# The first batch's value loads put behind the fourth unit's queries and keys

## The chip, the core and the metric

The kernel runs on one core of a Trainium2 chip. The metric is device time in microseconds (us) of one launch; lower is better. The core's engines are TensorE (PE; its weight loads are shown as PEld), VectorE (DVE), ScalarE (ACT), GpSimd (POOL) and SyncE (SP). SP issues all the transfers between the device memory and the core here, in the order of its queue, and sixteen DMA engines carry them.

## The reference

Windowed attention, and then a feed-forward layer with a maximum over three products:

```python
scores = q @ k.T / 8                       # 8 batches, 8 heads, 576 positions, 64 wide
# heads 0-3 see the last 32 positions; heads 4-7 every fourth of the last 128
attn = exp(masked - max) / (sum + 1e-9)
x = (attn @ v) as 4608 tokens x 512
h = max(x @ w1, x @ w2, x @ w3)            # 512 -> 768
out = h @ w_out                            # 768 -> 512
```

All is float32 with tight accuracy, so each product of the feed-forward layer is made of three: a high part and a low part of each operand are used (high times high, low times high, high times low).

## The kernel before, in words

**Units.** Attention is done in units of two heads: 8 batches of 4 units, `p` 0 to 3; `p` 0 and 1 are plain windows, 2 and 3 dilated. The first batch takes them in the order `PORDER = (2, 0, 3, 1)`, so the fourth unit is `p` 1. The first six units go through `full(b, p)`, the later ones through `attention` and `behind`. In names, `02` is batch 0, unit `p` 2, and `10` is batch 1, unit 0.

A unit of `full` loads its queries and keys (`fk`; the unit 03 has them in two, `fk` and `fq`) and its values (`fv`, two loads). On PE come the scores (`fs`, lines 576 and 582), transposes of the weights of attention (`ft`, 666 and 690) and the product with the values (`fpv`, 712). Between them ACT and DVE do the softmax, POOL multiplies by the reciprocal of the sum, and ACT copies the transposed tiles. At the end ACT and DVE write the unit's part of `x` as a high part `xH` and a low part `xL`.

**Weights.** The up weights are 18 pieces `st0` to `st17` of 512 KB, the down weights `st18` to `st24`. Each is loaded (line 473) and then split into high and low parts: ACT makes `cp` from `st` (446), POOL makes `c` from `st` (453), DVE joins them (459, 467), ACT writes `wupH` and POOL or DVE writes `wupL`. Piece `j` serves the group `u0_f_g` with `j = 3f + g`.

**Feed-forward.** Nine tiles of 512 tokens. A tile has 18 groups of 12 matmuls `u` (line 1021), which go in turn to two PSUM banks. The first of three groups is copied to `tmp` by ACT (`copy`, line 361), the next two are taken into the maximum by DVE (line 387); each of these frees the group's bank. ACT and POOL split the maximum into `h`. Then come 72 matmuls `d` (1092), and the output goes out (1121). In the first tile two groups, `u0_0_0` and `u0_0_1`, are done on three quarters of `x` before the fourth unit is ready, and then finished.

**What sets the order.** All steps are given to a `Plan`. `Plan.order` is a list scheduler: it has a cost for each step, a rate for the wire and due times, picks the next step of each engine, and so fixes the order of every engine's instructions and of SP's loads. A step becomes ready when the steps that it depends on have ended in the plan (`left` counts them, `next` lists who is waiting). `fill` steps are matmuls on zeros (line 1200, `idle`), put where the plan sees PE with nothing to do; the plan reckons with a slower PE after a stretch of little work (`TICK`, line 30, and lines 229 to 236). The instructions are then issued in that order, and each engine's queue is in that order. The waits on the chip come from data and buffers: a DMA that writes a buffer waits for the last reader, and an instruction waits for the landing of what it reads.

Queries and keys have two buffers (`k`) and the ones of unit 03 stand in two of six `h` buffers; the first batch's values take `h` buffers too. The pieces `st0` to `st22` use six `wd` buffers in turn.

Of the kernel before, what the change touches and what calls it, by code (L numbers as in the profile page):

```python
# [36 lines left out]
PORDER = (2, 0, 3, 1)  # L37
# [256 lines left out]
def tile_dilated_window_attention__then__maxout_ffn(  # L294
# [205 lines left out]
        return s, l, first  # L500


    first_of = [None] * (FULL + 1)

    def full(b, p):
# [18 lines left out]
        def load(dst, src, rows, n):  # L524
            return {"sp": 0.5}, lambda _: nc.sync.dma_start(out=dst.t[:rows, :n], in_=src), (), [dst], rows * n * 4 * PART[rows]

        if at_h:
            ks = plan.add(*load(kb, qk[b, p % 2, :, 576:], 128, nkc))
            heads = []
            qs = plan.add(*load(qb, qk[b, p % 2, :, :576], 128, 576))  # L530
        else:
            ks = qs = None
            heads = []
            heads.append(plan.add(*load(kb, qk[b, p % 2], 128, 576 + nkc)))
        if b:
            vs = []
            for i in range(2):
                n = at[i + 1] - at[i]

                def values_in(_, i=i, n=n):  # L540
                    dst = vb[i].t[:wk, : 2 * n * D].rearrange("p (j c) -> p j c", j=2)
                    nc.sync.dma_start(out=dst, in_=fv[b, p % 2, :, :, at[i] * D : at[i + 1] * D].rearrange("j p c -> p j c"))

                vs.append(plan.add({"sp": 0.5}, values_in, (), [vb[i]], wk * 2 * n * D * 4 * PART[wk]))
        else:
            vs = [plan.add(*load(vb[j], fv[b, p % 2, j], wk, 64 * nblk)) for j in range(2)]

        def value(n, j):

            if not b:  # L550
                return vb[j].t[:wk, D * n : D * n + D]
            i = n // 6
            c = D * (j * (at[i + 1] - at[i]) + n - at[i])
            return vb[i].t[:wk, c : c + D]
# [625 lines left out]
    for n in TILES:  # L1180
        plan.kind = "a"
        while HALF * 2 * (u // NPAIR) < t0 + n:
            for p in range(NPAIR):
                if u < FULL_UNITS:
                    plan.lead = UNIT_LEAD * (NPAIR - 1 - p)
                    x_of.extend(full(u // NPAIR, p if u >= NPAIR else PORDER[p]))
                else:
                    n_u = 1 if u < ALONE else 2
                    if u < ALONE or u % 2 == 0:
                        units(range(u, u + n_u))  # L1190
                u += 1
        plan.kind = "ffn"
        prev, last_up = ffn(t0, n, x_of, w_of, prev)
        readers.append((t0, t0 + n, last_up))
        t0 += n
# [72 lines left out]
```

## Time and profile before

| | |
|---|---|
| median of 3 runs | 687.71 us (687.3 to 687.76) |
| the profiled execution | 688.23 us, of which the span of instructions is 686.4 us |
| PE busy | 678.7 us, 99% of the span (the matmuls on zeros count as busy) |
| DVE, ACT, POOL busy | 335.3, 251.7, 179.5 us |
| moved by DMA | 55.43 MB; q1, SP's queue, 54.53 MB |

The profile's second part cuts the span in 40 slices of about 17 us and gives the busy share of each in tenths. Its timeline lists instructions with start, duration, engine, line, operation, output and inputs, and in brackets the idle time ahead of it and what ended it. A group of equal instructions on one engine is one row with a count.

### The profile page before, as it was taken

The page shows a single profiled execution, that of the slowest core. Times are in us where ns is not written, and L with a number is a line of the kernel's source. Part 1 is how long each engine was busy: PE and PEld are TensorE (multiplying, and loading weights), DVE is VectorE, ACT ScalarE, POOL GpSimd, SP SyncE. Part 2 cuts the span into 40 slices and gives each one's busy share as a digit, 9 for nine tenths or more (in the row PEclk, how much of TensorE's full clock was granted, in tenths as well). Part 3 has the DMA queues.
Part 4 walks back from the last instruction along what each step waited for, and adds up shares of the span by engine and source line. Part 5 has one row for each costly group of instructions (what it writes and reads, how often), then busy time and mean ns, then how long its engine had stood idle before and what let it go on. Part 6 is the DMA issues. An engine that isn't in the chain of part 4 may idle for free.

```text
span 686.4 us, 13901 instructions
## 1 busy us (share of the span) xinstructions
PE 678.7 (99%) x5458; PEld 552.1 (80%) x5458; DVE 335.3 (49%) x1194; ACT 251.7 (37%) x867; POOL 179.5 (26%) x228
## 2 busy tenths in 40 slices
PE   8999999999999999999999999999999999999997
PEld 5678778888888888888888888888888888888886
DVE  6879867786787675112765257614611211101110
ACT  5857665526534534112641254314311211111111
POOL 2657852323223412111232111311211001100110
PEclk9999999999999999999999999999999999999999
DMA  9997343141433123001610051101000000010001
GB/s 289 310 344 245 103 138 114 48 121 44 139 115 115 44 67 116 1 0 40 214 37 8 1 186 68 44 0 56 32 1 1 34 28 0 1 47 15 1 0 62
DMA packets 20690, 55.43 MB, mean 81 GB/s; under 512 B 2128, under 2 KB 6224, under 8 KB 20624
## 3 DMA queue, kind: packets, MB, share of 16 engines
q1 hardware_dynamic: 20624, 54.53, 24.0%
q8 instruction: 43, 0.70, 0.4%
q14 instruction: 23, 0.19, 0.1%
HBM read 45.09 MB, written 9.44 MB: 79 GB/s over the span
## 4 chain that ended last, share of the span: by engine, by line
PE 91%; DMA 4%; DVE 1%; POOL 1%; ACT 1%; issue 1%; SPq 0%; DVEq 0%; ACTq 0%; POOLq 0%
PE u L1021 60%; PE d L1092 22%; DMA st<-in_w_up_dram 4%; PE s L826 3%; PE pv L986 3%; PE idle L1200 1%; POOL W L387 1%; PE fpv L712 1%; PE ft L666 1%; ACT wupH L361 0%; DVE cp L459 0%; ACT cp L446 0%; DVE tmp L387 0%; DVE cp L467 0%; POOL h L387 0%
## 5 line engine op out<-in xcount | busy, mean ns | idle before, releaser
L387 DVE TENSOR_TENSOR tmp<-u,tmp 128x512 f32<-128x512 f32 x108 | 74.6, 691 | 251.8 <-PE u L1021 242.1
L1021 PE MATMUL u<-xH,wupH 128*128 128x512 f32 x648 | 175.3, 392 | 0.7 <-ACT tmp L361 0.5
L1021 PE MATMUL u<-xL,wupH 128*128 128x512 f32 x648 | 174.4, 391 | 0.0
L1021 PE MATMUL u<-xH,wupL 128*128 128x512 f32 x648 | 174.3, 390 | 0.0
L387 POOL TENSOR_TENSOR h<-tmp,h 128x512 fp32r<-128x512 f32 x54 | 69.9, 1295 | 322.9 <-ACT h L361 322.8
L1092 PE MATMUL d<-wdn,h 128*128 128x512 f32 x648 | 152.9, 393 | 0.0
L1021 PEld LDWEIGHTS u<-xH,wupH 128*128 128x128 f32 x648 | 120.7, 188 | 26.8 <-ACT tmp L361 1.4
L1021 PEld LDWEIGHTS u<-xL,wupH 128*128 128x128 f32 x648 | 121.2, 188 | 25.5
L1021 PEld LDWEIGHTS u<-xH,wupL 128*128 128x128 f32 x648 | 121.3, 188 | 25.3
L1092 PEld LDWEIGHTS d<-wdn,h 128*128 128x128 f32 x648 | 120.5, 188 | 26.0
L930 DVE STREAM_TRANSPOSE PT<-W 32x256 f32<-32x256 f32 (+2 forms) x320 | 120.2, 376 | 25.0 <-PE pv L986 9.7
L361 ACT CAST h<-tmp 128x512 fp32r<-128x512 f32 x54 | 33.5, 621 | 211.2 <-DVE tmp L387 211.2
L876 ACT ACTIVATE W<-W,mx 128x96 f32<-128x96 f32 x260 | 93.6, 364 | 22.2 <-DVE mx L864 19.5
L387 POOL TENSOR_TENSOR W<-W,sm 128x768 f32<-128x768 f32 (+2 forms) x52 | 49.6, 959 | 28.3 <-DVE sm L905 27.3
L361 ACT COPY tmp<-u 128x512 f32<-128x512 f32 x54 | 31.7, 586 | 67.0 <-POOL h L387 37.7
L864 DVE CUSTOM_DVE_ANT_0 W<-s,steps 128x96 f32<-128x96 f32 (+1 forms) x232 | 44.1, 252 | 12.0 <-PE s L826 11.6
L876 ACT ACTIVATION_READ_ACCUMULATOR W<-W,mx 128x1 f32 x260 | 49.5, 190 | 0.0
L361 ACT COPY o<-d 128x512 f32<-128x512 f32 (+1 forms) x36 | 21.0, 582 | 75.4 <-PE d L1092 64.2
L900 POOL TENSOR_TENSOR sm<-sm,small_c 128x8 f32<-128x8 f32 (+2 forms) x52 | 10.0, 196 | 108.6 <-ACT W L876 108.5
L361 ACT CAST xH<-pv 128x288 fp32r<-128x288 f32 (+8 forms) x70 | 20.2, 346 | 29.0 <-PE u L1021 20.8
L387 DVE TENSOR_TENSOR xL<-pv,xH 128x288 fp32r<-128x288 f32 (+8 forms) x70 | 23.0, 374 | 10.0 <-ACT xH L361 9.5
L986 PEld LDWEIGHTS pv<-PT,v 64*64 64x64 f32 x1152 | 22.1, 134 | 4.9 <-issue 4.6
(69 smaller groups left out, 350.6 us busy)
## 6 DMA issues: line engine op xcount, KB each, us to landing
st<-in_w_up_dram SPq DMA_DIRECT2D x18, 512.0 KB, 9.7
k<-in_qk_d_dram SPq DMA_DIRECT2D x14, 648.0 KB, 4.4
out_dram<-o SPq DMA_DIRECT2D x35, 256.0 KB, 2.0
k<-in_qk_p_dram SPq DMA_DIRECT2D x12, 592.0 KB, 4.3
v<-in_vw_d_dram SPq DMA_DIRECT2D x14, 384.0 KB, 3.3
v<-in_vw_p_dram SPq DMA_DIRECT2D x12, 320.0 KB, 3.7
st<-in_w_dn_dram SPq DMA_DIRECT2D x5, 512.0 KB, 4.5
fk<-in_qk_p_dram SPq DMA_DIRECT2D x4, 592.0 KB, 8.2
```

The source lines that it names most:

```text
L361: nc.scalar.copy(dst, src)
L387: (nc.vector if eng == "dve" else nc.gpsimd).tensor_tensor(dst, a, b, op=op)
L666: nc.tensor.transpose(flips[j].t[:wk, gw * g : gw * g + gw], W3(j)[:gw, g], ident[:gw, :gw])
L712: nc.tensor.matmul(pv[z].t[64 * j : 64 * j + 64, c : c + nq], value(n, j), turned(j, x, x + nq), start=True, stop=True,)
L826: nc.tensor.matmul(banks[j].t[o : o + nq, 96 * m : 96 * m + nk], kb.t[d, q0 : q0 + nq], kb.t[d, k0 : k0 + nk], start=True, stop=True,)
L864: nc.vector.tensor_tensor_reduce(W.t[rows, a], banks[j].t[rows, 96 * m : 96 * m + nk], mask_of(m)[rows], -0.125, 3e38, ALU.add, ALU.min, m ...
L876: nc.scalar.activation(W.t[rows, a], W.t[rows, a], AF.Exp, bias=mx.t[rows, n : n + 1], scale=-1.0, accum_out=sm.t[rows, n : n + 1],)
L900: nc.gpsimd.tensor_tensor(d, d, eps_c[rows].broadcast_to([d.shape[0], n]), op=ALU.add)
L930: plan.add({"dve": dve(32 * n) + 0.02}, lambda _: nc.vector.transpose(dst(), src()), [*deps, blank], [W, PT])
L986: nc.tensor.matmul(pv[z].t[64 * j : 64 * j + 64, q : q + c1 - c0], v.t[d, j, y], PT.t[d, 576 * j + 96 * x + c0 : 576 * j + 96 * x + c1], s ...
L1021: nc.tensor.matmul(sums(bank), wt[:, j, c, :], moving(xL if xz else xH, c), start=(m == 0 and c == EARLY[0]), stop=(m == 2 and c == EARLY[3]),
L1092: nc.tensor.matmul(bank.t, hs[f].t[:, hz, s0 : s0 + 128], wdn[f].t[:, wz], start=(f == 0 and m == 0), stop=(f == NF - 1 and m == 2),)
```

## The change

`full` collects the value loads of the first batch's four units. When the fourth unit (`p == PORDER[3]`) is added, each of these eight loads is made to depend, in the plan, on the load of that unit's queries and keys (`heads[0]`). The dependence is the plan's; no wait is written for the chip, beyond those of data and buffers.

```diff
+    first_vs = []
     first_of = [None] * (FULL + 1)
 
     def full(b, p):
...
         else:
             vs = [plan.add(*load(vb[j], fv[b, p % 2, j], wk, 64 * nblk)) for j in range(2)]
+            first_vs.extend(vs)
+            if p == PORDER[3]:
+                for st in first_vs:
+                    heads[0].next.append(st)
+                    st.left += 1
```

In rows of the changed kernel, lines 504 to 546 have become one higher, and those behind the change six higher.

The start of SP's queue, before (names end in a running number; `fk02` is 648 KB, an `fv0` load 240 or 216 KB, an `st` 512 KB):

```order
L525 DMA fk02_111<-in_qk_d_dram 128x1296
L525 DMA fk00_113<-in_qk_p_dram 128x1184
L525 DMA fv02_0_115<-in_fv_d_dram 80x768
L525 DMA fv02_1_121<-in_fv_d_dram 80x768
L525 DMA fk03_123<-in_qk_d_dram 128x720
L525 DMA fq03_165<-in_qk_d_dram 128x576
L525 DMA fv00_0_167<-in_fv_p_dram 96x576
L525 DMA fv00_1_195<-in_fv_p_dram 96x576
L525 DMA fk01_198<-in_qk_p_dram 128x1184
L473 DMA st0_207<-in_w_up_dram 128x512
L473 DMA st1_255<-in_w_up_dram 128x512
L525 DMA fv03_0_267<-in_fv_d_dram 80x768
```

And now:

```order
L526 DMA fk02_111<-in_qk_d_dram 128x1296
L526 DMA fk00_113<-in_qk_p_dram 128x1184
L526 DMA fk03_115<-in_qk_d_dram 128x720
L526 DMA fq03_121<-in_qk_d_dram 128x576
L473 DMA st0_123<-in_w_up_dram 128x512
L473 DMA st1_165<-in_w_up_dram 128x512
L526 DMA fk01_193<-in_qk_p_dram 128x1184
L473 DMA st2_229<-in_w_up_dram 128x512
L473 DMA st3_240<-in_w_up_dram 128x512
L473 DMA st4_247<-in_w_up_dram 128x512
L526 DMA fv02_0_294<-in_fv_d_dram 80x768
L526 DMA fv02_1_302<-in_fv_d_dram 80x768
```

Five pieces of the up weights and the fourth unit's queries and keys now stand ahead of the first values. The loads of `fv00`, `fv03`, `st5`, `fk10`, `fv01` and `fk11` follow, up to the 21st load, and behind them SP's queue differs a second time. Before, from the 22nd load on:

```order
L473 DMA st6_484<-in_w_up_dram 128x512
L542 DMA fv10_0_492<-in_fv_p_dram 96x2x384
L473 DMA st7_533<-in_w_up_dram 128x512
L473 DMA st8_552<-in_w_up_dram 128x512
L542 DMA fv10_1_569<-in_fv_p_dram 96x2x192
L473 DMA st23_573<-in_w_dn_dram 128x256
L473 DMA st24_581<-in_w_dn_dram 128x256
L473 DMA st9_606<-in_w_up_dram 128x512
```

Now, from the 22nd on:

```order
L473 DMA st6_474<-in_w_up_dram 128x512
L543 DMA fv10_0_518<-in_fv_p_dram 96x2x384
L473 DMA st7_526<-in_w_up_dram 128x512
L543 DMA fv10_1_545<-in_fv_p_dram 96x2x192
L473 DMA st23_550<-in_w_dn_dram 128x256
L473 DMA st24_565<-in_w_dn_dram 128x256
L543 DMA fv11_0_575<-in_fv_p_dram 96x2x384
L473 DMA st8_604<-in_w_up_dram 128x512
L473 DMA st9_614<-in_w_up_dram 128x512
```

`st8` moved from the 25th place to the 29th: `fv10_1`, `st23`, `st24` and `fv11_0` now stand ahead of it, and no load that stood ahead of it before has moved behind it.

ACT's queue around `cp8`, the instruction that reads `st8`, before:

```order
L446 ACTIVATE cp7_698<-st7_533 128x512
L361 CAST wupH_76<-c6_616 128x512
L446 ACTIVATE cp8_713<-st8_552 128x512
L361 COPY tmp0_0_719<-u0_0_0_564 128x512
L361 CAST wupH_76<-cp7_698 128x512
```

And now:

```order
L446 ACTIVATE cp7_630<-st7_526 128x512
L361 CAST wupH_76<-c4_548 128x512
L446 ACTIVATE cp8_669<-st8_604 128x512
L361 CAST wupH_76<-cp5_578 128x512
L361 COPY tmp0_0_685<-u0_0_0_561 128x512
```

The copy of the first group, which frees its bank for `u0_0_2`, stands behind `cp8` in both; now a cast stands between the two.

On PE the two scores steps of units 10 and 11 stood ahead of `u0_0_1`. Now the scores of unit 10 stand behind the first nine matmuls of `u0_0_1`, and those of unit 11 stand within `u0_3_1`, the eleventh group. Ahead of the first `u`, the second half of the transposes of unit 00 now stands ahead of the value product of unit 02, and from that product on there are 14 `idle` matmuls where there were 15. SP's load of `k13` moved from the 36th place to the 45th, behind all the weights.

## The prediction

> **What bounds the kernel now.** I read the page first, then busy times by stage, then PE's timeline of the first 50 us, and then the rows of ACT and SP that the change moves. The page's first row, and the slices of PE and of the DMA engines:
>
> ```profile
> PE 678.7 (99%) x5458; PEld 552.1 (80%) x5458; DVE 335.3 (49%) x1194; ACT 251.7 (37%) x867; POOL 179.5 (26%) x228
> PE   8999999999999999999999999999999999999997
> DMA  9997343141433123001610051101000000010001
> ```
>
> PE is the bound: from the second slice on it has work all the time. DVE at 49% tells nothing of a single stage. The DMA engines are full in the first three slices alone, which is where the change is. By stages (length, then busy time and count of PE, PEld, DVE, ACT, POOL; granted clock, DMA share, GB/s):
>
> ```profile
> 5.00:40.00 35.00, 32.88 (x531) 23.42 (x530) 29.11 (x58) 23.87 (x69) 18.71 (x21) 1.00 1.04 313
> 40.00:60.00 20.00, 19.48 (x85) 15.47 (x84) 16.10 (x26) 12.70 (x23) 13.19 (x15) 1.00 0.98 340
> 60.00:100.00 40.00, 40.00 (x393) 31.78 (x392) 32.94 (x101) 27.33 (x88) 26.84 (x31) 1.00 0.40 131
> ```
>
> Up to 40 us the DMA share is 1.04: loads wait in line, and one put ahead delays all behind it. From 60 us PE has no gap, so what it loses before that stays lost to the end. PE's timeline around the first groups, `idle` being matmuls on zeros:
>
> ```profile
> 18.96 1.60 PE L712 MATMUL fpv<-PT,fv 80*64 80x48 f32 x48
> 30.25 0.93 PE L1021 MATMUL u<-xH,wupH 128*128 128x512 f32 x3
> 33.80 0.58 PE L576 MATMUL fs<-steps,identb 128*128 128x96 bf16 x4
> 35.29 0.58 PE L576 MATMUL fs<-steps,identb 128*128 128x96 bf16 x4
> 40.08 0.39 PE L1021 MATMUL u<-xH,wupL 128*128 128x512 f32 x1
> 40.52 1.19 PE L1021 MATMUL u<-xH,wupH 128*128 128x512 f32 x4
> 43.37 1.07 PE L1021 MATMUL u<-xH,wupH 128*128 128x512 f32 x4
> 46.09 1.07 PE L1021 MATMUL u<-xH,wupH 128*128 128x512 f32 x4
> 47.91 1.07 PE L1021 MATMUL u<-xH,wupL 128*128 128x512 f32 x4
> 49.44 1.19 PE L1021 MATMUL u<-xH,wupH 128*128 128x512 f32 x4 [0.46 <-ACT tmp L361]
> ```
>
> The real feed-forward work begins at 30.25 (`u0_0_0`). `u0_0_2` begins at 40.52, and then a group comes every 2.72 us (43.37 to 46.09). `u0_1_2` is late: it was due at 47.91 + 0.91 = 48.82 and came at 49.44, so 0.62 us lost. It waited for ACT's copy of `u0_1_0`. ACT's rows show why:
>
> ```profile
> 38.07 0.64 ACT L446 ACTIVATE cp<-st 128x512 f32<-128x512 f32 x1 [0.18 <-DMA st<-in_w_up_dram]
> 39.88 0.59 ACT L361 COPY tmp<-u 128x512 f32<-128x512 f32 x1 [1.17 <-PE u L1021]
> 47.77 0.63 ACT L446 ACTIVATE cp<-st 128x512 f32<-128x512 f32 x1 [1.75 <-DMA st<-in_w_up_dram]
> 48.34 0.58 ACT L361 CAST wupH<-cp 128x512 fp32r<-128x512 f32 x1
> 48.81 0.58 ACT L361 COPY tmp<-u 128x512 f32<-128x512 f32 x1
> ```
>
> `u0_1_0` was complete when `u0_1_1` began at 46.09, yet its copy ran at 48.81. ACT takes its queue in order and stood 1.75 us at `cp11`, waiting for a piece of weights, with the copy two places behind. The chain that ended last, in this stretch, consists of those two landings:
>
> ```profile
> 28.45 9.59 DMA st<-in_w_up_dram
> 38.13 9.61 DMA st<-in_w_up_dram
> ```
>
> So `st8`, issued at 28.45, landed at 38.04, and `st11` at 47.74. From the landing of `st11` to the group that it held, 49.44, took 1.70 us: `cp`, a cast, the copy, in that order. That price is used below.
>
> **The change, part by part.** It adds no instruction of arithmetic; it moves loads in SP's queue and, through the plan, the order on all engines.
>
> *The first values.* `fv02` now stands behind `st0` to `st4`. The four pieces `st2` to `st5` were issued in one row, the third of them, `st4`, at about 14.1:
>
> ```profile
> 13.18 1.85 SPq L473 DMA_DIRECT2D st<-in_w_up_dram  x4
> st<-in_w_up_dram SPq DMA_DIRECT2D x1, 512.0 KB, 10.4
> ```
>
> It landed 10.4 us later, at 24.5. All that stands ahead of `fv02` now stood ahead of `st4` or was `st4`; `fv00` and `fv03` (912 KB) have gone behind. At 313 GB/s they are 3.0 us, so `fv02` lands at about 21.5 and its product runs 2.5 us later than at 18.96. From there to the first `u` was 30.25 - 18.96 = 11.3 us; some 0.8 us of transposes and one zero matmul now stand ahead of it or are gone, which leaves 10.2. The first `u` comes at about 31.7, 1.4 us later, if the plan's zero matmuls cover the rest as before.
>
> *The scores of unit 11* move from ahead of `u0_0_1` to the eleventh group. One scores step is 35.29 - 33.80 = 1.49 us. So PE is ready for `u0_0_2` at 31.7 + (40.08 + 0.23 - 30.25) - 1.49 = 40.3, no later than before, but it owes 1.49 us.
>
> *`st8`* is the step that decides. Four loads now stand ahead of it that stood behind: `fv10_1`, `st23`, `st24`, `fv11_0`, 944 KB. Their issues, and the times to landing of `st24`, `st9` and `fv11_0`:
>
> ```profile
> 29.30 0.93 SPq L473 DMA_DIRECT2D st<-in_w_dn_dram  x2
> 31.61 0.33 SPq L473 DMA_DIRECT2D st<-in_w_up_dram  x1
> 33.80 0.33 SPq L542 DMA_DIRECT2D fv<-in_fv_p_dram  x1
> st<-in_w_dn_dram SPq DMA_DIRECT2D x1, 256.0 KB, 10.4
> st<-in_w_up_dram SPq DMA_DIRECT2D x1, 512.0 KB, 10.9
> fv<-in_fv_p_dram SPq DMA_DIRECT2D x1, 288.0 KB, 10.0
> ```
>
> `st24`, the second of the pair, landed at 29.8 + 10.4 = 40.2, `st9` at 42.5, `fv11_0` at 43.8. So the first three took 40.2 - 38.04 = 2.15 us and `fv11_0` 1.3, together 3.4; at 313 GB/s the 944 KB would be 3.1. I take 3.4, since these are the loads themselves: `st8` lands at 41.4.
>
> [...]
>
> ACT holds the copy of `u0_0_0` behind `cp8` and a cast, the same three instructions that took 1.70 us behind `st11`. Before, the copy had slack: `st8` was there at 38.04, and it waited for PE until 39.88. Now `u0_0_2` begins at 41.4 + 1.7 = 43.1, not 40.52: 2.6 us later. With the 1.49 us owed that is 4.1. The 0.62 us lost at `u0_1_2` come back: the bank of `u0_1_0` is now needed at about 51.4, three groups after 43.1, and `st11`, which has lost the 648 KB load of `k12` from ahead of it, lands no later than before. The sum is 3.5 us.
>
> *PE's clock.* PE stands from 40.3 to 43.1 with no zero matmuls in that place. The rows of the start and the end:
>
> ```profile
> 0.99 3.60 PE L1200 MATMUL idle<-blank_b 128*128 128x512 bf16 x8 [0.99 <-DVE blank_b L317]
> 7.84 2.33 PE L1200 MATMUL idle<-blank_b 128*128 128x512 bf16 x10
> 681.30:684.70 3.40, 0.98 (x5) 0.48 (x3) 0.42 (x1) 0.37 (x1) 0.00 (x0) 1.00 0.15 52
> 684.75:686.40 1.65, 0.00 (x0) 0.00 (x0) 0.00 (x0) 0.00 (x0) 0.00 (x0) 0.50 0.12 42
> ```
>
> Eight matmuls took 3.60 us at the start, 0.45 each, and ten took 2.33 later, 0.23 each. At the end the clock fell to 0.50 at 684.75, after a stretch of 3.4 us with 0.98 of work in it. A stand of 2.8 us is as poor a stretch. If the clock falls, one spell of slow matmuls like that at the start costs up to 8 x (0.45 - 0.23) = 1.7 us; nothing if it doesn't, and less if part of the spell falls into the stand. I take 1.4, nearer the upper end. Sum: 3.5 + 1.4 = 4.9 us.
>
> [...]
>
> *What hides the rest.* Two steps of DVE in a busy stretch, POOL's product for the transposes of unit 10, and these on PE:
>
> ```profile
> 50.15 0.69 DVE L459 SCALAR_TENSOR_TENSOR cp<-cp,c 128x512 uint32<-128x512 uint32 x1
> 50.75 0.68 DVE L387 TENSOR_TENSOR tmp<-u,tmp 128x512 f32<-128x512 f32 x1
> 67.73 1.94 POOL L387 TENSOR_TENSOR W<-W,fsm 128x480 f32<-128x480 f32 x2 [1.52 <-DVE fsm L645]
> 69.67 0.61 PE L666 MATMUL ft<-ident,W 128*96 128x128 f32 x4
> ```
>
> While ACT is held, DVE has nothing to do but to wait for the copy. From there it has about 40 steps at 0.6 us each, 24 us, before POOL can make that product, and PE reaches the transposes ten groups and a scores step later, 29 us. If that cover is gone, these transposes are late next: before, POOL ended just as PE came to them. Loads of weights that wait on DVE's reads are late by some us, with their groups 10 us or more away. `k13`, now behind all of them, is read near the end of the first tile, some 20 us later. These I cost at nothing.
>
> Against the profiled execution's own 688.23 us this makes 693.1. That execution is 0.5 above the median of 687.71, so for the median I forecast 692.6.
>
> **Rivals.** *Slower, and the clock holds.* For it: 2.8 us is short of the 3.4 us stretch, and a border in the middle of it leaves two half-busy stretches. Against it: the fall at 684.75. Then 3.5 us: 691.2, from 690.9 with `st8` 3.1 us late to 692.
>
> *Not slower: the early weights pay.* `st0` to `st4` land several us earlier and can be split before DVE is full. If `fv02` is no later than PE's need, the first `u` starts at 18.96 + 10.2 = 29.2, and `u0_0_2` 37.8 at the earliest; with the 1.49 us owed and the 0.62 back that is 1.9 us won, 685.8. It decides at the landing of `st8`: the full gain needs 37.8 - 1.7 = 36.1, at 38.0 nothing is won or lost, and up to 39.3 the loss stays within 0.2%. For it: some transposes and a zero matmul fewer on PE's way to the first `u`. Against it: four more loads in a queue with a share of 1.04. That the change does not do what it says belongs here too: SP's order shows the values behind other loads, not held until one has landed. The values may then be early enough, but `st8` is behind its four loads all the same.
>
> *Much slower.* A second stand, at the transposes of unit 10 or a second slow spell: 2 us more, 694.6 and up.
>
> **How the numbers follow.** The forecast's own case has 0.47, the rival without the fall 0.28, not slower 0.17, much slower 0.08. The range from 690.0 to 694.6 holds the first two and part of the last, 0.8. What a measurement can tell from no change is about 0.2%, 1.4 us. Slower by more than that is the first, second and fourth, 0.83; of the third, 0.05 is faster by over 0.2% (below 686.3), 0.12 within.
>
> **What the changed profile would show.** SP's rows: `st8` issued as the 29th load and landing at 41 to 42. ACT: idle at `cp8` until then, some 3 us, by "DMA st". PE: no row between about 40.3 and 43, then `u0_0_2` with "ACT tmp" as what ended it; 0.45 us for a matmul of 512 columns in the next 3.4 us and a granted clock below 1.00 there. Then no gap; the chain holds `st8`. Wrong: if `st8` lands before 39, or PE stands at the values of unit 02 far beyond 21.5, or a later gap shows.

## The result, and the profile after

The changed kernel took 694.12 us, median of 4 runs (692.86 to 695.22), against 687.74 (also 4 runs) for the kernel before: ratio 1.0093, 95% interval 1.0070 to 1.0116. It is slower. The four runs are two pairs, 692.86 and 693.14, 695.10 and 695.22; the profile is of the slowest, with a span of 693.4 us (before: 686.4).

The page of the changed kernel, busy times and the slices of PE, of its granted clock and of the DMA engines:

```profile
PE 682.3 (98%) x5457; PEld 555.4 (80%) x5457; DVE 335.4 (48%) x1195; ACT 253.4 (37%) x867; POOL 179.1 (26%) x227
PE   8889999999999999999999999999999999999997
PEclk9989999999999999999999999999999999999999
DMA  9977343231243102001531042101000000010001
```

PE was busy 3.6 us longer with one matmul fewer: the same work took longer. The clock row has an 8 in the third slice (35 to 52 us). PE's timeline:

```profile
20.09 1.60 PE L718 MATMUL fpv<-PT,fv 80*64 80x48 f32 x46 [0.77 <-DMA fv<-in_fv_d_dram]
31.61 0.96 PE L1027 MATMUL u<-xH,wupH 128*128 128x512 f32 x3
40.01 0.40 PE L1027 MATMUL u<-xH,wupL 128*128 128x512 f32 x1
43.17 2.07 PE L1027 MATMUL u<-xH,wupH 128*128 128x512 f32 x4 [2.77 <-ACT tmp L361]
45.04 1.91 PE L1027 MATMUL u<-xL,wupH 128*128 128x512 f32 x4
46.75 1.91 PE L1027 MATMUL u<-xH,wupL 128*128 128x512 f32 x4
48.45 1.42 PE L1027 MATMUL u<-xH,wupH 128*128 128x512 f32 x4
51.52 1.07 PE L1027 MATMUL u<-xH,wupH 128*128 128x512 f32 x4
54.24 1.07 PE L1027 MATMUL u<-xH,wupH 128*128 128x512 f32 x4
68.75 0.58 PE L582 MATMUL fs<-steps,identb 128*128 128x96 bf16 x4
70.24 1.19 PE L1027 MATMUL u<-xL,wupH 128*128 128x512 f32 x4
```

All but two matmuls of the product with the first values begin at 20.09, and the first real group at 31.61. PE has done all it can before `u0_0_2` at 40.01 + 0.40, and stands 2.77 us until 43.17 for ACT's copy (`tmp`). Then three groups take 54.24 - 43.17 = 11.07 us, where three of 2.72 would be 8.16. From 54.24 on the pace is the usual one, and at 68.75 come the scores of unit 11, 1.49 us, which the kernel before had done ahead of `u0_0_1`. ACT's rows at that stand:

```profile
41.50 0.62 ACT L446 ACTIVATE cp<-st 128x512 f32<-128x512 f32 x1 [3.91 <-DMA st<-in_w_up_dram]
42.06 0.58 ACT L361 CAST wupH<-cp 128x512 fp32r<-128x512 f32 x1
42.53 0.58 ACT L361 COPY tmp<-u 128x512 f32<-128x512 f32 x1
```

ACT waits 3.91 us at `cp8` for the landing of `st8`; the cast and the copy follow, and 1.67 us after ACT goes on PE does too. The chain that ended last holds that landing:

```profile
32.76 8.72 DMA st<-in_w_up_dram
```

So `st8`, issued at 32.76, landed at 41.48. What PE's clock did, in four neighbouring stretches of 3.41 us (the columns: length, busy time and count of PE, PEld, DVE, ACT, POOL, then granted clock, DMA share, GB/s):

```profile
38.94:42.35 3.41, 1.46 (x6) 0.85 (x5) 0.00 (x0) 0.85 (x2) 0.65 (x2) 1.00 1.02 366
42.35:45.77 3.42, 2.60 (x6) 2.12 (x7) 2.58 (x5) 2.49 (x5) 2.58 (x3) 0.50 1.01 403
45.77:49.18 3.41, 3.41 (x9) 2.63 (x9) 1.09 (x3) 0.59 (x1) 0.70 (x2) 0.50 0.64 233
49.18:52.59 3.41, 3.41 (x16) 2.82 (x16) 3.31 (x6) 2.63 (x5) 2.46 (x2) 1.00 0.16 61
```

After a stretch in which PE had 1.46 us of work the clock was 0.50 for two stretches, 9 matmuls in the second of them against 16 at full clock. PE's last group of `d` in the two kernels, from the chain that ended last, first before, then after (where it begins is called PE's end below):

```profile
665.94 16.36 PE d L1092 x72
```

```profile
672.25 16.36 PE d L1098 x72
```

So PE ends 6.31 us later. The span grew by 7.0. The other 0.7 us lie behind PE's last matmul. The last microseconds of the DMA engines, before and after:

```profile
out_dram<-o SPq DMA_DIRECT2D x2, 128.0 KB, 1.8
```

```profile
q14 instruction: 1, 0.01, 0.3%
out_dram<-o SPq DMA_DIRECT2D x2, 128.0 KB, 2.3
```

The last two output transfers land 2.3 us after their issue instead of 1.8, and one packet of program code (q14) lies among them.

### The profile page after: what moved, and what is told of

Its sections match the earlier page's. It is cut to its first block, busy times and chain, and to the rows that moved or that the text cites. A ratio compares the mean times of both kernels' runs of the same rounds, so it can differ in the third digit from the quotient of the medians.

```text
span 693.4 us, 13895 instructions
## 1 busy us (share of the span) xinstructions
PE 682.3 (98%) x5457; PEld 555.4 (80%) x5457; DVE 335.4 (48%) x1195; ACT 253.4 (37%) x867; POOL 179.1 (26%) x227
## 4 chain that ended last, share of the span: by engine, by line
PE 95%; DMA 3%; DVE 0%; SPq 0%; ACT 0%; issue 0%; ACTq 0%
PE u L1027 64%; PE d L1098 22%; PE s L832 3%; PE pv L992 3%; DMA fv<-in_fv_d_dram 2%; DMA st<-in_w_up_dram 1%; PE fpv L718 1%; PE idle L1206 1%; PE ft L672 0%; PE fs L588 0%; SPq L473 0%; PE ft L696 0%; PE fs L582 0%; SPq L526 0%; DVE c L467 0%
## 5 line engine op out<-in xcount | busy, mean ns | idle before, releaser
L361 ACT COPY tmp<-u 128x512 f32<-128x512 f32 x54 | 31.7, 587 | 67.5 <-POOL h L387 34.8
L361 ACT CAST xH<-pv 128x288 fp32r<-128x288 f32 (+8 forms) x70 | 20.5, 348 | 31.9 <-PE u L1027 20.8
```

Source lines behind the costliest of these rows:

```text
L361: nc.scalar.copy(dst, src)
```

## Experiments

All are edits of one of the two kernels. Those that move loads leave every other engine's order alone:

```diff
     def issue(self, fill=None):
-        for st in self.order(fill):
+        steps = self.order(fill)
+        for side, names, at in self.MOVES:
+            moved = [st for st in steps if st.name in names]
+            steps = [st for st in steps if st.name not in names]
+            i = next(i for i, st in enumerate(steps) if st.name == at) + (side == "behind")
+            steps[i:i] = moved
+        for st in steps:
```

The kernel before, run beside them on the same chip, had medians of 688.15, 688.34 and 687.90 us in the three sets, so ratios are compared rather than times.

**Theory A**: ACT is held at `cp8` by the landing of `st8`, PE stands, and its clock may fall. **Rival B**: the late first values cost the time. **Rival C**: the changed order on PE, ACT and DVE does.

**e1: `st8` back, in the changed kernel**

```diff
+    MOVES = [("behind", ("fv10_1", "st23", "st24", "fv11_0"), "st8")]
```

> The changed kernel with one thing undone in SP's queue: fv10_1, st23, st24 and fv11_0 stand behind st8 again; the late first values and the plan's order on the other engines stay. Theory A (ACT is held at cp8 by the landing of st8, PE stands, and its clock falls): st8 lands at about 38, u0_0_2 begins at 40.5 to 41.0 instead of 43.17, no stretch at half clock from 42 on, and what is left is the 1.49 us of scores done later less the 0.62 won back at u0_1_2: 688.3 to 689.5 us. Rival B (the late first values cost the time) and rival C (the changed order on PE, ACT and DVE does): st8 lands early, but the time stays at 692.5 to 695.

Measured: 691.55 us (690.65 to 693.46), ratio 1.0047 (1.0028 to 1.0066). ACT's row at `cp8`, PE's timeline, and the chain's last group of `d`, in its fastest execution (690.65):

```profile
38.02 0.65 ACT L455 ACTIVATE cp<-st 128x512 f32<-128x512 f32 x1 [0.65 <-DMA st<-in_w_up_dram]
```

```profile
40.99 1.20 PE L1043 MATMUL u<-xH,wupH 128*128 128x512 f32 x4
49.40 1.19 PE L1043 MATMUL u<-xH,wupH 128*128 128x512 f32 x4
```

```profile
667.55 16.36 PE d L1114 x72
```

`st8` was there at 38.02, ACT waited 0.65 us for it, and `u0_0_2` came at 40.99, as foreseen; PE's end is 1.61 us behind the kernel before instead of 6.31. Between these two executions 4.70 us go with the landing of `st8` and the clock behind it. Between the medians it is less: 1.0047 against 1.0093, or against 1.0068 where the changed kernel was measured again (e8). The time missed its forecast by 2 us, and the runs spread, most of the slower ones at a lower mean clock (0.997 to 0.992). In the profiled execution PE's pace halved at the product with the late first values: behind 3.41 us with 1.46 us of work, up to 21.52, four transposes took 0.97 us (from 22.70), and 0.55 again from 25.01. So these cost something through the clock when `st8` is early.

**e2: `st8` late, in the kernel before**

```diff
+    MOVES = [("ahead", ("fv10_1", "st23", "st24", "fv11_0"), "st8")]
```

> The kernel before with that one part of the change alone: fv10_1, st23, st24 and fv11_0 stand ahead of st8 in SP's queue, all else as before. Theory A: st8 lands 3 us later, at 41 to 41.7, u0_0_2 begins at 42.7 to 43.4 instead of 40.52 (+2.2 to +2.9), 0.62 us come back at u0_1_2: 689.3 to 690 if the clock holds, 692 to 693 if two windows of 3.4 us at half clock follow as in the changed kernel. Rivals B and C: 687.4 to 688.2, since neither the first values nor the order on the engines is touched.

Measured: 689.89 us (688.70 to 692.25, 12 runs), ratio 1.0019 (1.0004 to 1.0034). PE's timeline, and two stretches of 3.41 us:

```profile
42.88 1.44 PE L1037 MATMUL u<-xH,wupH 128*128 128x512 f32 x4 [1.97 <-ACT tmp L370]
52.78 1.07 PE L1037 MATMUL u<-xH,wupH 128*128 128x512 f32 x4
```

```profile
40.23:43.64 3.41, 1.44 (x6) 0.89 (x6) 0.78 (x2) 1.62 (x3) 1.75 (x2) 1.00 1.03 406
43.65:47.06 3.41, 3.41 (x9) 2.67 (x8) 2.25 (x4) 1.74 (x3) 2.48 (x4) 0.50 1.03 414
```

That part alone makes the stand, 1.97 us, and after a stretch with 1.44 us of work the clock falls, here for one. Eight of the twelve runs have a mean clock of 0.999 or 1.000 and average 689.46 us; four have 0.996 or 0.997 and average 691.70. One kernel, two times, and the mean clock goes with them. B and C allowed no change here; the interval just excludes none.

**e3: the first values back, `st8` late, in the changed kernel**

```diff
+    MOVES = [("ahead", ("fv02_0", "fv02_1"), "fk03")]
```

> The changed kernel with the other thing undone: fv02_0 and fv02_1 stand ahead of fk03 in SP's queue again, st8 stays behind its four loads. Theory A: the first product with values comes some 2 us earlier and the first u 1 to 2 us earlier than 31.61, but u0_0_2 still waits for st8 and begins at 42.8 to 43.4; PE only stands longer, and the clock falls as well: 692.5 to 695.5. Rival B: what the first u gains reaches the end: 1.4 us or more below the changed kernel, 691.5 to 692.7.

Measured: 694.21 us (691.22 to 694.59), ratio 1.0070 (1.0049 to 1.0092).

```profile
30.67 0.96 PE L1043 MATMUL u<-xH,wupH 128*128 128x512 f32 x3
43.65 2.07 PE L1043 MATMUL u<-xH,wupH 128*128 128x512 f32 x4 [4.19 <-ACT tmp L370]
```

The first `u` came 0.94 us earlier than 31.61, and PE merely stood longer, 4.19 us; `u0_0_2` came at 43.65, 0.25 later than the latest that was foreseen. The ratio lies between the two of the changed kernel, 1.0093 and 1.0068 (e8), so the time alone does not exclude B; the longer stand does.

**e7: both back, so that the order on the engines and of the other loads is left**

```diff
+    MOVES = [("behind", ("fv10_1", "st23", "st24", "fv11_0"), "st8"), ("ahead", ("fv02_0", "fv02_1"), "fk03")]
```

> The changed kernel with both ends of SP's queue put back: fv02_0 and fv02_1 ahead of fk03, and fv10_1, st23, st24, fv11_0 behind st8. What is left of the change is the order that the plan gave to PE, ACT, DVE and the other loads. Theory A: no stretch at half clock, u0_0_2 begins at 40 to 40.8, and 1.49 us of scores are owed less 0.62: 688.3 to 689.5 us. Rival C (the order on the engines costs more than that): 690.5 or more.

Measured: 690.06 us (688.93 to 691.80, 11 runs), ratio 1.0026 (1.0016 to 1.0037), 1.8 us. PE's timeline and the chain:

```profile
40.41 1.20 PE L1043 MATMUL u<-xH,wupH 128*128 128x512 f32 x4 [2.27 <-ACT tmp L370]
49.24 1.20 PE L1043 MATMUL u<-xH,wupH 128*128 128x512 f32 x4 [0.37 <-ACT tmp L370]
```

```profile
667.37 16.36 PE d L1114 x72
```

Only `fv02` went back, and the other first values still stand behind the weights. PE stood 2.27 us ahead of `u0_0_2` here too, held by `st8`, past which ACT went on at 38.74. `u0_1_2` comes at 49.24, 0.20 earlier than before; with the scores owed, 1.49, that is 1.29, and PE's end is 1.43 later. So what is left of the change costs the scores that it puts off, and the tail its 0.7. The time is 0.6 above the top of the expectation, of which 0.6 is the kernel before being slower in this set. It is also 0.4 below what rival C gave. "No stretch at half clock" held in the profiled execution, but five of the eleven runs have a mean clock of 0.996 or 0.997, as e2's profiled execution has with one slow stretch, and they are not the slower ones: they average 689.75, the other six 690.66. Why was not found.

The four kernels with the changed order now stand in a square, as ratios: values late and `st8` late 1.0068 (e8; 1.0093 when first measured), values early and `st8` late 1.0070, values late and `st8` early 1.0047, both early 1.0026. So a late `st8` costs 0.0044, 3.0 us, with early values, and 0.0021, 1.4 us, with late ones (3.2 us by 1.0093). Late values cost some 1.4 us where `st8` does not hide them, though the intervals of 1.0047 and 1.0026 overlap.

**e8: the changed kernel again**, unedited.

> The changed kernel once more, on the same chip as the three others. Theory A: its runs lie in two or three steps of some 1.7 us, by how many windows of 3.4 us at half clock fall into the stand ahead of u0_0_2, between 691 and 695.5 us. Rival: one narrow group of runs.

Measured: 693.04 us (692.66 to 694.11, 5 runs), ratio 1.0068 (1.0056 to 1.0080). The profiled execution took 692.80. Its PE timeline, two stretches, and the chain:

```profile
33.38 0.96 PE L1027 MATMUL u<-xH,wupH 128*128 128x512 f32 x3
43.52 1.19 PE L1027 MATMUL u<-xH,wupH 128*128 128x512 f32 x4 [1.35 <-ACT tmp L361]
51.79 1.07 PE L1027 MATMUL u<-xH,wupH 128*128 128x512 f32 x4
```

```profile
20.61:24.02 3.41, 3.41 (x49) 3.04 (x46) 0.92 (x2) 0.95 (x3) 0.47 (x1) 0.50 1.06 211
41.09:44.50 3.41, 2.06 (x9) 1.40 (x8) 1.00 (x2) 2.66 (x5) 1.73 (x3) 1.00 1.01 401
```

```profile
669.82 16.36 PE d L1098 x72
```

This is the same program as the 695.22 us execution. Here the clock was at 0.50 early, from 20.61 to 27.44, at the product with the late first values. The first `u` came 1.8 us later, at 33.38, and `u0_0_2` only 0.35 later: PE reached it later and stood 1.35 us instead of 2.77, the stretch around the stand had 2.06 us of work, and the clock did not fall there. Three groups took 51.79 - 43.52 = 8.27 us instead of 11.07. PE's end is 669.82 - 665.94 = 3.88 us behind the kernel before, and 2.43 ahead of the other execution. Four of the five runs lie within 0.4 us, as the rival had it, and none came near 695; the run of 694.11 fits neither group and was not profiled. Two sorts of run show only with the first four taken in.

**e5, e6, e9, e10: zero matmuls in the stand.** To test the clock by itself, matmuls on zeros are added into the bank of `u0_0_1`, ahead of its last matmul (twelve in e5; in the other three 12, 0 and 20, and five more ahead of the product with the first values):

```diff
                 def up(_, m=m, wt=wt, xz=xz):
+                    if not t0 and j == 1 and m == 2 and chunks == EARLY[3:]:
+                        for _ in range(12):
+                            nc.tensor.matmul(
+                                bank.t.rearrange("p (n k) -> p n k", n=4),
+                                blank_b,
+                                blank_b.unsqueeze(1).broadcast_to([128, 4, 128]),
+                                start=False,
+                                stop=False,
+                            )
                     for c in chunks:
...
+        zeros = {"pv02": 5}     # e6, e9, e10
         for st in steps:
+            for _ in range(zeros.get(st.name, 0)):
+                fill.fn(fill.eng)
```

> The changed kernel with twelve matmuls on zeros (512 columns, added into the bank of u0_0_1, which nobody reads for another 3 us) just ahead of that group's last matmul, so that PE works through the stand ahead of u0_0_2. No load and no wait is touched. If PE's clock falls because PE stands (theory A): u0_0_2 still begins at 43.0 to 43.4, held by ACT's copy, but no stretch at 0.50 follows, the next three groups take 2.72 us each, u0_1_2 begins at 51.2 to 51.6 instead of 54.24, and the time is 690.7 to 691.8 us. Rival (the clock falls there whatever PE does, or zeros don't count as work): half clock after 42 as in the changed kernel, 692.9 to 695.2.

> As the kernel with twelve zero matmuls ahead of u0_0_2, and five more ahead of the product with the first values of unit 02, where PE stood 0.97 and 0.77 us and the clock fell at 21.87. Theory A: that stretch goes too; since it lay beside waits it cost little, so 690.3 to 691.6 us, 0 to 0.6 below the kernel with the twelve alone, and the runs lie closer together. Rival (the early slow stretch is a main cost): 1.5 us or more below the kernel with the twelve alone. Other rival: the five delay the product by their 1.1 us and all behind it: 0.5 to 1.1 above it.

> The changed kernel with five zero matmuls ahead of the product with the first values of unit 02 and none ahead of u0_0_2. The early ones keep the early slow stretch away, so PE is at u0_0_2 by 38.7, and stands there with nothing to do until ACT's copy, 43.2 to 44.2. If PE's clock falls because PE stands (theory A), it falls in nearly every run, at 40 to 44, for one or two windows of 3.4 us: the time is 1.7 to 2.9 us above 693.5 (what the kernel with five and twelve took in its runs with no slow stretch), 695 to 696.5, and the mean clock 0.993 to 0.998. Rival (a slow stretch there has nothing to do with how much PE has in hand): the same 693.5 to 695 and the same mix as with twelve.

> The same with twenty zero matmuls (4.6 us) instead of none ahead of the last matmul of u0_0_1, so that PE stands less than 1.2 us. No load and no wait is touched. Theory A: no slow stretch in any run (mean clock 0.999 to 1.000), u0_0_2 at 43.2 to 44.2 as before, and 693.0 to 694.0 us; what is left over the kernel before is st8's landing, the scores owed and the tail. Rival: slow stretches as with none, 694.5 or more; or the zeros run past ACT's copy and delay u0_0_2 by up to 0.5.

Measured: 694.30 (e5, 693.18 to 694.72), 693.85 (e6, 691.72 to 695.13), 693.97 (e9, 692.23 to 697.68) and 693.44 us (e10, 693.05 to 694.63). The first three medians lie outside what theory A gave. That of e10 lies inside, but `u0_0_2` came late and only two of its five runs had the mean clock that was forecast, 0.999 or more. The profiles say why. In e5 no early slow stretch held PE back, it came to the stand at 38.5, and the twelve zeros were done well before ACT's copy. Of the stretch before the fall they left this (in e6's it was some 0.9 us of work, an estimate from PE's rows: they begin at 44.16, and their pace halves at about 45.1, with 1.91 us for four matmuls from 45.29 and 1.07 from 48.60):

```profile
40.30:43.72 3.42, 1.35 (x7) 0.58 (x6) 0.19 (x1) 1.84 (x4) 1.07 (x2) 1.00 1.03 411
```

In e9, with no zeros there, an early slow stretch came in spite of the five (0.97 us for the four transposes at 22.51, 0.58 in e5), PE reached the stand at 41.2, and the stretch around its beginning had more work; the clock held, at 1.00 until 46.11:

```profile
39.29:42.70 3.41, 1.91 (x18) 1.17 (x10) 0.35 (x1) 0.57 (x2) 0.95 (x2) 1.00 1.03 388
```

In e10 the stand was full (3.41 us of work from 40.14 to 43.55) and the clock held, at 1.00 until 46.96, but the zeros ran past ACT's copy, and `u0_0_2` came at 45.32 instead of 43.2 to 44.2; an early slow stretch came here as well, with 0.95 us for the four transposes at 23.41 against 0.58 at 22.39:

```profile
40.76 4.49 PE L1049 MATMUL u<-blank_b 128*128 128x512 bf16 x20
45.32 1.09 PE L1057 MATMUL u<-xH,wupH 128*128 128x512 f32 x4
```

What can be taken from them: with none, two of six runs have a mean clock of 0.993 and take 695.10 and 697.68; with twenty all five lie between 0.997 and 0.999 and within 1.6 us. That fits theory A, but two of six against none of five is too few to show it, and the medians, 693.97 and 693.44, hardly differ. So what brings the clock down is not shown by these four. In e6 four of six runs had a clock of 0.999 or more, so nearly no slow stretch, and still took 691.72 to 694.11 against 688.34. The loss without the clock is real.

**e4 and e11: removing the 0.62 us at `u0_1_2` from the kernel before**

```diff
+    MOVES = [("behind", ("fv10_1", "st23", "st24", "fv11_0", "k12"), "st11")]     # e4
+    MOVES = [("behind", ("k12",), "st11")]                                        # e11
```

> The kernel before with fv10_1, st23, st24, fv11_0 and k12 put behind st11 in SP's queue, so that st11 lands some 4 to 5 us earlier than 47.74. If ACT's stand at cp11 is what held the copy of u0_1_0 (theory A's reading of the 0.62 us), the gap ahead of u0_1_2 goes: 687.0 to 687.3. Rival: the gap stays, because something else ends it (the copy's own place, or a later piece), or the five loads are late themselves: 687.6 or more.

> The kernel before with one load moved in SP's queue: k12 (648 KB) behind st11 instead of ahead of the piece after it, the other loads in place. st11 lands up to 1.6 us earlier, at 46.2 to 47.7. If it does, ACT's stand at cp11 is shorter and the 0.62 us ahead of u0_1_2 go, with no later piece moved back (which is what took them away again when five loads were moved): 0.3 to 0.7 us below the kernel before. Rival: k12 stands behind st11 already, or st11's landing is set by its buffer: no change, within 0.3.

Measured: 688.74 us, ratio 1.0001 (0.9990 to 1.0013), for e4; 688.80, ratio 1.0014 (1.0000 to 1.0027), for e11. In both the gap at `u0_1_2` is gone. In e4 there is one of 1.21 us three groups later, behind a later piece that ACT waited for; the rows of PE and ACT:

```profile
49.42 1.07 PE L1037 MATMUL u<-xH,wupH 128*128 128x512 f32 x4
58.95 1.20 PE L1037 MATMUL u<-xH,wupH 128*128 128x512 f32 x4 [1.21 <-ACT tmp L370]
```

```profile
54.94 0.64 ACT L455 ACTIVATE cp<-st 128x512 f32<-128x512 f32 x1 [1.78 <-DMA st<-in_w_up_dram]
```

In e11's profiled execution (687.89 us) the gain stayed; PE's timeline and the chain:

```profile
49.41 1.07 PE L1037 MATMUL u<-xH,wupH 128*128 128x512 f32 x4
```

```profile
665.57 16.36 PE d L1108 x72
```

There is no idle time ahead of 49.41. `u0_0_2` had come 0.56 us later than before, at 41.08, so 0.59 of the 0.62 us are back, and PE's last group of `d` begins 0.37 us earlier than 665.94. In the median the runs are no faster than the kernel before, though. No version beat it.

## Why the prediction was right, and where it was off

The time, 694.12, is 1.5 above the forecast of 692.6 and inside the range. By the steps of the prediction, in us, for the two profiled executions of the changed kernel:

| step | forecast | in the 695.22 execution | in the 692.80 execution |
|---|---|---|---|
| first `u` | 31.7 | 31.61 | 33.38 |
| ACT goes on at `cp8` | 41.4 | 41.50 | 41.84 |
| `u0_0_2` later by | 2.6 | 43.17 - 40.52 = 2.65 | 43.52 - 40.52 = 3.00 |
| scores of unit 11 owed | 1.49 | 1.49 | 1.49 |
| back at `u0_1_2` | -0.62 | -0.62 | -0.62 |
| PE's clock behind the stand | 1.4 | 11.07 - 8.27 = 2.80 | 0 |
| sum, and PE's end later by | 4.9 | 6.32, 6.31 | 3.87, 3.88 |
| behind PE's last matmul | 0 | 0.69 | 0.68 |

*`st8`* was the step that decides, and it was right in place, wait and size: four loads ahead of it by their own times to landing (3.44 us, 41.48 against 38.04; 3.4 forecast), then three instructions of ACT at 1.7 us. e1 and e2 show it from both sides. *Scores owed* is shown by e7 within 0.14 us. *0.62 back* is seen in both executions of the changed kernel, where the groups run on without a gap; in e7 a gap of 0.37 us stayed. That it hung on `st11` is shown by e4 and e11. The effects that the prediction costed at nothing ahead of PE's last matmul were nothing: the sums close within 0.01 us.

*The clock* is the term that was mis-sized. "One spell of slow matmuls costs up to 1.7 us" reckoned with one stretch; where the clock fell in the changed kernel it fell for two, of which the first held the end of the stand and 2.60 us of work in six slow matmuls, and 2.80 us were lost. In the other group it did not fall at all behind `u0_0_2`. The 1.4 hit the middle of a quantity that was 0 or 2.8, and that is luck: one slow spell behind the stand, the forecast's own case, is in neither profile of the changed kernel (e2, e3 and e5 have it). The two groups are two other cases of the prediction by their mechanism: "slower, and the clock holds" behind the stand, though later than its 691.2, for the most part by 0.7 of tail and 0.4 at `u0_0_2` (692.7 to 693.1 measured), and "much slower", a second slow spell (694.6 and up; 695.1 and 695.2 measured). Of the nine runs six are of the first sort by time, close to the forecast's 692.6 by another way. That they and the run of 695.10 went as the profiled execution of their sort did is inferred from their times; the mean clocks, 0.994 or 0.995 and 0.993, hardly tell the sorts apart.

In the 695.22 execution the clock changed at 21.87, 25.29, 42.35 and 49.18, all on one grid of 3.41 us, and the grid lies elsewhere in other executions (43.65 in e2, 43.72 in e5). The stretch ahead of a fall was not without work: 1.46, 1.44 and 1.35 us (the changed kernel, e2, e5) did not keep the clock up.

*The first values*: the first `u` was forecast to the tenth, but by luck. Their product began at 20.09, not 21.5, and from there to the first `u` took 11.5 us, not 10.2; the two errors cancel. The longer way has in it a slow stretch, 21.87 to 25.29: that PE's clock would fall there too was not foreseen. With `st8` late it is nearly hidden and may shorten the stand (e8); e1 against e7 puts the late values at some 1.4 us where it is not.

*The tail*, 0.7 us, was costed at nothing by silence. With the changed order PE's last group of `d` begins 21.1 to 21.4 us ahead of the end (the changed kernel, e1, e3, e7, e8, e10), with the order before 20.5 to 20.6 (the kernel before, e2, e4, e11). The last two output transfers land 2.2 or 2.3 us after their issue in the changed kernel, e1, e3 and e8, and 1.7 or 1.8 us after it in the kernel before, e2 and e4. A packet of code (q14) starts 2.4 us ahead of the end in the changed kernel; one moves in the last 6 us of e8 and in the last 19 us of e1, and none in the last 16 us of the kernel before, the last 5 of e2 and the last 18 of e4. Whose code it is, and that the packet is what delays them, was not tested.

"Not slower: the early weights pay" failed at the point that the text names: `st8` landed at 41.5, not by 39.3. And the values were, as that rival said, not held until the queries and keys had landed: SP issued the first at 8.03, and the fourth unit's scores waited for their queries and keys until 13.08.

The 313 GB/s at which the prediction prices loads, a mean from 5 to 40 us, is no ceiling: five rows above show 401 to 414 GB/s over 3.41 us.

## What to carry to other kernels

A dependence given to a planner moves more than the load it names: read the new queue for what now stands ahead of the load that an in-order engine waits for, and price it by those loads' own landings. A stand on the path has two prices, its length and what the clock does after it; here the second was 2.80 us in one execution and nothing in another of the same program, so forecast it as two cases and not as their mean. A delay ahead of a wait that ends later anyway is nearly free: 1.8 us at the first `u` became 0.35 at the wait (e8).

## What the runs showed of the hardware

At the stand, PE's clock fell after a window of 3.41 us with 0, some 0.9, 1.35, 1.44 and 1.46 us of PE work (e3, e6, e5, e2, the changed kernel) and held after 1.91 and 2.06 (e9, e8). Busy time is not the whole measure: ahead of the changed kernel's early slow stretch there was more of it, in small matmuls, and the clock fell:

```profile
18.46:21.87 3.41, 2.10 (x51) 1.92 (x52) 2.06 (x5) 1.49 (x6) 2.47 (x3) 1.00 1.05 235
```

In e10 it fell after some 2.5 us in 54 matmuls, an estimate from its rows up to 22.81, and in e5 it held after 2.00 in 15 (16.41 to 19.82); what it goes by stays open. At half clock a window with 2.60 us of 512-column matmuls did not bring it back (the changed kernel, 42.35 to 45.77), the next, with 3.41, did; 3.41 us of mostly small ones (e8, 49 matmuls, 20.61 to 24.02) did not. And one packet of code at the end (the 23 of the whole execution are 0.19 MB, some 8 KB each) goes with 0.7 us.
